# Four engines pinned to the written order instead of five: SyncE's transfers left to the scheduler

## The chip, the cores and the metric

One core of one Trainium2 chip runs the whole program. The metric is device microseconds (us) of that core. A core has four computing engines, called here as the profile calls them: PE (TensorE, matrix multiplication), DVE (VectorE), ACT (ScalarE) and POOL (GpSimd). The fifth, SP (SyncE), computes nothing in this kernel: it issues transfers (DMAs) between the main memory and the on-chip memory. Each engine works through its own list of instructions in a fixed order. An instruction whose inputs are not there yet holds up everything behind it in the same list, on SP as on the others.

## What is computed

Two stages follow each other, all in float32. The first is an attention with a complex decay, for 4 batches and 8 heads, 768 steps, 48 channels:

```python
mag = np.sqrt(a_re * a_re + a_im * a_im)
scale = np.minimum(mag, 0.999) / (mag + 1e-06)
a_re_n, a_im_n = (a_re * scale, a_im * scale)
for t in range(S):
    new_re = ar * S_re - ai * S_im
    new_im = ar * S_im + ai * S_re
    S_re, S_im = (new_re + kv, new_im)          # kv: outer product of k[t] and v[t]
    y[:, :, t] = einsum(q[:, :, t], S_re)
```

The second takes y as x of shape (4, 768, 384) and computes a gated product: a causal convolution over 5 steps and a sigmoid give `gate`, and the output is `(gate * (x @ w_val)) @ w_out`.

## The kernel before, in words

The heads are cut into 10 units, in the order in which they are worked on: units 0, 1, 8 and 9 have 2 heads each, units 2 to 7 have 4. A unit needs five inputs, `ar`, `ai`, `k`, `q` (each loaded by two transfers of line 114) and `v` (three transfers, line 132). The steps of one unit are these:

- `prep_x` (from line 269) turns `ar` and `ai` into logarithms and angles. ACT reads `ar` at line 278 and DVE reads `ai` at line 284; each frees the buffer that it read.
- Sums, angles, sines and exponentials follow (lines 304 to 367).
- `prep_b` (from line 369): DVE multiplies by `k` (line 379) and makes the tile `kx` (line 382); SP writes `kx` to a scratch tensor `kd` in main memory (line 392, two transfers). Then DVE multiplies by `q` (line 379) and makes `qx` in the tile `trig` (line 382).
- `load_kn` (from line 402) reads `kd` back in another layout into a tile `kn`, in two sets for each unit (line 413; two or three transfers each). A set can begin when `kd` has landed and one of three `kn` buffers is free. The transfers of one set write interleaved columns of one tile, and the second waits until the first has landed.
- `transpose` (from line 416): PE transposes `kx` and `qx` (line 430), ACT copies the results into `kq` (line 431). There is one `kx` buffer, so the next unit's `kx` waits until these transposes are done.
- `Attend` works through six chunks of 128 steps: scores on PE (lines 457 and 458), mask on DVE (line 464), output on PE (lines 477 and 480, copied by ACT at 481), and the running state from `kn` and `v` on PE (lines 494 and 495, copied by ACT at 497). `collect` (line 509, issued by POOL) moves the output into the layout of the second stage, whose convolution is on DVE (lines 518 and 521), sigmoid on ACT (529), and products on PE (line 255).

The four inputs `ar`, `ai`, `k`, `q` share six buffers (`LB`, line 80), and `v` has two (`VB`). When the trace of the program is recorded, each step is written in the order of the long string `ORDER` (line 22): one letter is one step of one stream, for instance `L` a load, `N` a `kn` set, `V` a load of `v`. In `move` (line 795) a load is written only after the step that read the buffer six loads earlier. The buffer that it really gets is chosen later, by the scheduler of the framework, among those that are free.

That scheduler goes through the recorded instructions and gives each engine its list. Left alone it puts, on each engine, the instruction first that is ready first by its own estimate of times, and the one written first among those ready. The lines 855 to 866 take this freedom away: they go through all instructions and tie each one to the one before it on the same engine, if the engine is in `IN_ORDER` (lines 35 to 37). Such a tie costs no semaphore on the chip; it fixes the order of the list only.

```python
IN_ORDER = (
    mybir.EngineType.PE, mybir.EngineType.Activation, mybir.EngineType.DVE, mybir.EngineType.SP, mybir.EngineType.Pool
)
```

Of the kernel before, what the change touches and what calls it, by code (L numbers as in the profile page):

```python
# [32 lines left out]
    "MDMOOMMMMMOCCCCCCGMMMMMMMMOOMMO"  # L33
)
IN_ORDER = (
    mybir.EngineType.PE, mybir.EngineType.Activation, mybir.EngineType.DVE, mybir.EngineType.SP, mybir.EngineType.Pool
)
TURN = 2.0 ** 24
RADIAN = 2.0 * PI / 2.0 ** 32 * (1.0 - 2.0 ** -22)
# [962 lines left out]
```

## Time and profile before

| what | value |
|---|---|
| median of 3 runs | 351.83 us (351.12 to 354.74) |
| time of the profiled execution | 351.17 us |
| its span, first to last instruction | 349.4 us |
| PE, DVE, ACT, POOL busy | 269.5, 257.9, 245.7, 60.1 us |
| mean granted clock of PE | 0.924 of full speed |
| moved by DMA | 53.31 MB |

The profile is one execution. "Busy" is the time in which an engine computes; SP has none, so its rows show when it issues transfers. An idle time is shown in brackets with what ended it. "SPq" is SP's list, "L114" is line 114 of the kernel, and `kn<-kd` reads "written: `kn`, read: `kd`". A row with x3 in SP's rows spans three transfers, from the issue of the first to the end of the issue of the third.

### The profile page before, as it was taken

To read this page: it belongs to the slowest core of one execution; us is meant where nothing else is said; L and a number is where in the kernel's file an instruction comes from. 1 tells how busy PE (TensorE), PEld (TensorE's weight loads), DVE (VectorE), ACT (ScalarE), POOL (GpSimd) and SP (SyncE) were. 2 spreads that over 40 slices of the span, in tenths; PEclk is the share of its full clock that TensorE was granted. 3 is DMA by queue.
4 is the path that set the end of the run, shared out by engine and by line. 5 is a ranking of instruction groups with operands and counts; after the bars stand their busy time and mean duration, and the time that the engine had idled before them with its cause. 6 is when DMAs were issued, how large, how long until landed. Compare 5 with 4: busy or idle time off the path is not lost.

```text
span 349.4 us, 8122 instructions
## 1 busy us (share of the span) xinstructions
PE 269.5 (77%) x3234; PEld 210.8 (60%) x3234; DVE 257.9 (74%) x341; ACT 245.7 (70%) x455; POOL 60.1 (17%) x148
## 2 busy tenths in 40 slices
PE   0033757668977999996669999979989999999960
PEld 0023646538866777576458787668779666766530
DVE  4799869995959999929297899577769956476400
ACT  5758789999657899987357989956996457553110
POOL 3000001111023032020212022200342031240210
PEclk9999887956989999999968999996999999999995
DMA  7993576768697851595969403768950441530220
GB/s 203 316 224 112 140 231 182 108 207 221 172 239 200 167 169 48 193 272 170 258 127 208 108 33 102 218 176 259 191 139 26 124 105 46 154 93 2 85 68 7
DMA packets 87804, 53.31 MB, mean 153 GB/s; under 512 B 36432, under 2 KB 84816, under 8 KB 87760
## 3 DMA queue, kind: packets, MB, share of 16 engines
q1 hardware_dynamic: 83664, 43.28, 48.8%
q0 software_dynamic: 4096, 9.44, 9.1%
q8 instruction: 27, 0.44, 0.5%
q14 instruction: 17, 0.14, 0.1%
HBM read 33.83 MB, written 14.16 MB: 137 GB/s over the span
## 4 chain that ended last, share of the span: by engine, by line
DMA 24%; DVE 19%; PE 18%; ACT 16%; issue 9%; SPq 8%; POOL 2%; POOLq 0%; DVEq 0%; ACTq 0%
DMA kn<-kd 14%; SPq L114 4%; ACT L104 4%; PE pt L430 3%; PE pv L255 3%; PE po L255 3%; ACT kq L431 3%; DVE sm L464 3%; DVE z L521 2%; DMA kd<-kx 2%; DVE kx L382 2%; DVE main L379 2%; DMA raw<-in_moe_w_val_dram 2%; SPq L413 2%; PE sc_ps L457 2%
## 5 line engine op out<-in xcount | busy, mean ns | idle before, releaser
L509 POOL DMA_DIRECT2D xT<-y_sb x80 | 40.8, 516 | 156.3 <-ACT y_sb L481 120.8
L431 ACT COPY kq<-pt 96x384 f32<-96x384 f32 x128 | 51.8, 508 | 4.4 <-PE pt L430 4.2
L521 DVE SCALAR_TENSOR_TENSOR z<-xT,cw_sb,z 128x768 f32<-128x768 f32 (+1 forms) x60 | 51.4, 856 | 1.7
L480 PE MATMUL y_ps<-sm,v_in 128*48 128x128 f32 x384 | 44.0, 294 | 10.2 <-DVE sm L464 10.2
L255 PE MATMUL po<-wo_sb,z 128*64 128x384 f32 x288 | 51.2, 488 | 0.0
L255 PE MATMUL pv<-xT,wv_sb 128*64 128x384 f32 x288 | 49.8, 486 | 0.0
L464 DVE TENSOR_TENSOR sm<-sc_ps,mask 128x512 f32<-128x512 f32 (+1 forms) x60 | 34.5, 578 | 15.9 <-PE sc_ps L458 11.8
L430 PE MATMUL pt<-ident,kx 128*96 128x128 f32 x192 | 37.9, 314 | 9.8 <-DVE kx L382 9.5
L457 PE MATMUL sc_ps<-kq 96*64 96x128 f32 x384 | 43.2, 286 | 1.7 <-DVE sm L464 1.7
L477 PE MATMUL y_ps<-kq,S_sb 96*48 96x128 f32 x320 | 38.5, 300 | 7.3 <-ACT y_sb L481 5.1
L458 PE MATMUL sc_ps<-kq 96*64 96x64 f32 x384 | 43.3, 229 | 0.0
L458 PEld LDWEIGHTS sc_ps<-kq 96*64 96x64 f32 x384 | 40.1, 143 | 2.0
L104 ACT ACT_TABLE_LOAD x31 | 39.8, 1283 | 1.3 <-PEq L986 0.8
L430 PE MATMUL pt<-ident,trig 128*96 128x128 f32 x192 | 36.7, 306 | 4.7 <-DVE trig L382 2.8
L457 PEld LDWEIGHTS sc_ps<-kq 96*64 96x64 f32 x384 | 33.6, 145 | 4.6 <-DVE sm L464 2.1
L255 PEld LDWEIGHTS pv<-xT,wv_sb 128*64 128x64 f32 x288 | 25.8, 137 | 16.1
L494 PE MATMUL S_ps<-v_in,kn 128*64 128x48 f32 x320 | 30.0, 233 | 7.2 <-ACT S_sb L497 5.1
L480 PEld LDWEIGHTS y_ps<-sm,v_in 128*48 128x48 f32 x384 | 28.6, 133 | 11.2 <-DVE sm L464 11.2
L481 ACT COPY y_sb<-y_ps 112x256 f32<-112x256 f32 (+1 forms) x60 | 19.5, 324 | 21.9 <-PE y_ps L480 21.6
L255 PEld LDWEIGHTS po<-wo_sb,z 128*64 128x64 f32 x288 | 24.6, 136 | 15.4 <-DVE z L542 1.5
L430 PEld LDWEIGHTS pt<-ident,kx 128*96 128x96 f32 x192 | 24.1, 144 | 14.4 <-issue 11.9
L477 PEld LDWEIGHTS y_ps<-kq,S_sb 96*48 96x48 f32 x320 | 22.6, 132 | 15.6 <-ACT y_sb L481 8.1
(84 smaller groups left out, 487.6 us busy)
## 6 DMA issues: line engine op xcount, KB each, us to landing
kd<-kx SPq DMA_DIRECT2D x12, 576.0 KB, 4.4
out_dram<-ot POOLq DMA_DIRECT2D x24, 192.0 KB, 2.5
ar_in<-in_a_re_dram SPq DMA_DIRECT2D x12, 288.0 KB, 4.5
ai_in<-in_a_im_dram SPq DMA_DIRECT2D x12, 288.0 KB, 5.2
k_in<-in_k_dram SPq DMA_DIRECT2D x12, 288.0 KB, 4.4
q_in<-in_q_dram SPq DMA_DIRECT2D x12, 288.0 KB, 4.4
xT<-y_sb POOLq DMA_DIRECT2D x48, 72.0 KB, 3.2
v_in<-in_v_dram SPq DMA_DIRECT2D x16, 144.0 KB, 5.1
```

The costliest lines, as they stand in the source:

```text
L104: nc.scalar.preload_act_table_set(name)
L255: nc.tensor.matmul(out[c:c + 64], lhsT[:, c:c + 64], rhs, **kw)
L430: nc.tensor.transpose(pt[:C2, j, :], src[:, j, f, h, :], ident)
L431: nc.scalar.copy(tj[:, s, f], pt[:C2].rearrange("c j p -> c p j"))
L457: nc.tensor.matmul(sc[lo:lo + half, h, :], k[:, :half], q, start=True, stop=True)
L458: nc.tensor.matmul(sc[hi:hi + half, h, half:], k[:, half:], q[:, half:], start=True, stop=True)
L464: nc.vector.tensor_tensor(out=two(sm), in0=two(sc[:, :g]), in1=mask[:, :, None, :].to_broadcast([C, 2, g // 2, C]), op=ALU.mult)
L477: nc.tensor.matmul(o, self.S_sb[n - 1][:, h * D:(h + 1) * D], self.part(1, h, n), start=True, stop=False)
L480: nc.tensor.matmul(o, vt[:, h, n], sm[:, h, :], start=(n == 0), stop=True)
L494: nc.tensor.matmul(S_all[:64, cols], kn[:, c0:c0 + 64], vt[:, h, n], **at_h)
L509: XQ.dma_start(out=xTs[b][c0 % P:c0 % P + c2 - c0, c0 // P, EXT + hf * HS:EXT + (hf + 1) * HS], in_=self.y[hf][r0:r0 + c2 - c0, h // 2],)
L521: nc.vector.scalar_tensor_tensor(out=z, in0=xT[:, c, EXT + t0 - t:EXT + t0 - t + n], scalar=cw_sb[:, TAPS - 1 - t, c:c + 1], in1=z, op0=AL ...
```

## The change

SP is taken out of `IN_ORDER`. The loop of lines 855 to 866 then leaves out SP's instructions, and their order is chosen by the scheduler: at each point of its own estimated time, of the transfers that are ready, the one written first. What a transfer waits for (its data, its buffer) stays as it was. PE, ACT, DVE and POOL keep the written order. No instruction is added or removed.

```diff
 IN_ORDER = (
-    mybir.EngineType.PE, mybir.EngineType.Activation, mybir.EngineType.DVE, mybir.EngineType.SP, mybir.EngineType.Pool
+    mybir.EngineType.PE, mybir.EngineType.Activation, mybir.EngineType.DVE, mybir.EngineType.Pool
 )
```

## Rows read from the trace of the kernel before

**Rows 1.** The chain of work that ended last, on the page: its shares of the span by line.

```profile
DMA kn<-kd 14%; SPq L114 4%; ACT L104 4%; PE pt L430 3%; PE pv L255 3%; PE po L255 3%; ACT kq L431 3%; DVE sm L464 3%; DVE z L521 2%; DMA kd<-kx 2%; DVE kx L382 2%; DVE main L379 2%; DMA raw<-in_moe_w_val_dram 2%; SPq L413 2%; PE sc_ps L457 2%
```

**Rows 2.** Waits of SP's own list over the whole span: line, what it waited for, us in total, times, longest.

```profile
SPq L413 <- DMA kn<-kd: 70.3, 20, 6.9
SPq L392 <- DVE kx L382: 44.0, 3, 23.6
...
SPq L392 <- DVE z L542: 18.1, 1, 18.1
...
SPq L114 <- ACT kq L431: 1.8, 2, 1.2
```

**Rows 3.** Waits of all computing engines over the whole span, the two that name a load: us in total, times, longest.

```profile
DVE main L284 <- DMA ai_in<-in_a_im_dram: 21.4, 5, 6.3
...
ACT main L278 <- DMA ar_in<-in_a_re_dram: 13.1, 6, 4.5
```

**Rows 4.** SP's list in order of time: start us, us, line, transfer, count.

```profile
92.48 1.05 SPq L114 DMA_DIRECT2D ar_in<-in_a_re_dram  x2
...
97.34 2.46 SPq L392 DMA_DIRECT2D kd<-kx  x2
...
102.75 8.60 SPq L413 DMA_DIRECT2D kn<-kd  x3
...
122.16 1.00 SPq L114 DMA_DIRECT2D ar_in<-in_a_re_dram  x2
140.85 1.23 SPq L392 DMA_DIRECT2D kd<-kx  x2
144.24 4.33 SPq L413 DMA_DIRECT2D kn<-kd  x3
148.63 1.22 SPq L114 DMA_DIRECT2D ai_in<-in_a_im_dram  x2
...
155.77 8.05 SPq L413 DMA_DIRECT2D kn<-kd  x3
...
165.20 2.72 SPq L114 DMA_DIRECT2D ai_in<-in_a_im_dram  x2
168.03 9.00 SPq L413 DMA_DIRECT2D kn<-kd  x3
177.12 3.68 SPq L132 DMA_DIRECT2D v_in<-in_v_dram  x3
...
219.87 4.25 SPq L413 DMA_DIRECT2D kn<-kd  x3
224.18 1.10 SPq L114 DMA_DIRECT2D ai_in<-in_a_im_dram  x2
```

**Rows 5.** DVE in order of time, the readers of `ai` (L284), `k` and `q` (L379) and the makers of `kx` (L382): start us, us, in brackets the idle time before.

```profile
109.32 1.35 DVE L284 TENSOR_TENSOR main<-tmp,ai_in 128x1152 f32<-128x1152 f32 x1
...
136.88 1.35 DVE L379 TENSOR_TENSOR main<-main,k_in 128x1152 f32<-128x1152 f32 x1
138.26 2.56 DVE L382 TENSOR_TENSOR kx<-trig,main 128x2304 f32<-128x2304 f32 x1
...
141.21 1.35 DVE L379 TENSOR_TENSOR main<-main,q_in 128x1152 f32<-128x1152 f32 x1
...
154.62 1.36 DVE L284 TENSOR_TENSOR main<-tmp,ai_in 128x1152 f32<-128x1152 f32 x1 [6.34 <-DMA ai_in<-in_a_im_dram]
...
157.34 2.56 DVE L382 TENSOR_TENSOR kx<-trig,main 128x2304 f32<-128x2304 f32 x1
...
174.28 1.36 DVE L284 TENSOR_TENSOR main<-tmp,ai_in 128x1152 f32<-128x1152 f32 x1 [6.02 <-DMA ai_in<-in_a_im_dram]
```

**Rows 6.** ACT in order of time, three readers of `ar`.

```profile
49.02 1.16 ACT L278 ACTIVATE main<-ar_in 128x1152 f32<-128x1152 f32 x1 [1.63 <-DMA ar_in<-in_a_re_dram]
...
97.46 1.16 ACT L278 ACTIVATE main<-ar_in 128x1152 f32<-128x1152 f32 x1 [3.42 <-DMA ar_in<-in_a_re_dram]
...
236.59 0.68 ACT L278 ACTIVATE main<-ar_in 128x576 f32<-128x576 f32 x1 [4.53 <-DMA ar_in<-in_a_re_dram]
```

**Rows 7.** Busy time by stretch of 35 us: the stretch, its us, PE, PEld, DVE, ACT and POOL busy with their instructions, granted clock of PE, share of the DMA engines, GB/s.

```profile
105.00:140.00 35.00, 31.99 (x414) 25.12 (x412) 34.10 (x37) 31.30 (x52) 7.16 (x16) 1.00 0.59 145
140.00:175.00 35.00, 27.83 (x363) 20.77 (x358) 22.21 (x21) 24.96 (x45) 6.28 (x14) 0.98 0.79 223
```

**Rows 8.** Waits of PE from 140 to 186 us: us in total, times, longest.

```profile
PE y_ps L480 <- DVE sm L464: 6.5, 2, 4.9
PE S_ps L494 <- DMA v_in<-in_v_dram: 2.0, 2, 1.0
...
PE S_ps L495 <- DMA kn<-kd: 0.5, 1, 0.5
```

**Rows 9.** Waits of PE from 70 to 116 us, the one on `kn`.

```profile
PE S_ps L495 <- DMA kn<-kd: 3.5, 2, 2.7
```

**Rows 10.** PE in order of time: the end of unit 4's transposes, and three instructions with idle time before them.

```profile
98.88 0.34 PE L494 MATMUL S_ps<-v_in,kn 128*64 128x48 f32 x1 [2.57 <-ACT S_sb L497]
...
153.65 0.53 PE L430 MATMUL pt<-ident,trig 128*96 128x128 f32 x3
...
234.75 0.42 PE L480 MATMUL y_ps<-sm,v_in 128*48 128x128 f32 x3 [2.11 <-DVE sm L464]
...
237.53 0.34 PE L494 MATMUL S_ps<-v_in,kn 128*64 128x48 f32 x1 [0.68 <-ACT S_sb L497]
```

## The prediction

> **What bounds the kernel now.** I began with the chain of work that ended last [rows 1]. Its largest single piece is not a computation but the read-back `kn<-kd`, 14% of the span, and SP's list stands in it by name (L114, L413). So I went to the waits of SP's own list [rows 2]. The reader should see two long ones. SP stood 70.3 us at line 413, in 20 waits, until the first transfer of a `kn` set had landed so that the second could follow. And it stood at line 392 until DVE had made a `kx`: 44.0 us and 18.1 us in the two largest entries. While SP stands, nothing behind it goes out, whether it is ready or not. The third view says who pays [rows 3]: DVE waited 21.4 us for `ai`, ACT 13.1 us for `ar`.
>
> Then the stretches. From 105 to 140 us DVE is full (34.10 of 35 us); from 140 to 175 us no engine is: PE 27.83, DVE 22.21, ACT 24.96 [rows 7]. Where all three are idle at once, something outside them sets the pace, and SP's list shows what: after the load of `ar` at 122.16 it stands until the store of `kx` at 140.85, then issues a `kn` set, and only at 148.63 the load of `ai` for which DVE then idles 6.34 us [rows 4, 5].
>
> **Could the load have gone earlier?** It needs a free buffer. The written rule would give it the one of six loads before, which is `q` of unit 4, read at 141.21 [rows 5]. But the rule is not what the chip waits for: the `ar` load at 122.16 went out although the `k` that the rule names was read only at 136.88 [rows 4, 5]. So any free buffer serves, and the last one needed was freed when DVE had read the previous `ai`, at 109.32 + 1.35 = 110.67. The load issued at 148.63 could go right behind the `ar` load, at about 123: 25 us earlier. Likewise the `ai` loads at 165.20 and 224.18 could follow the reads at 154.62 and 174.28 (the first of these itself earlier by then). None of these loads depends on the store or the set that it now stands behind.
>
> **The change part by part.** It removes no transfer and adds none: the issue time on SP stays, about 0.6 us for each transfer (1.22 us for the two at 148.63 [rows 4]), and it is hidden since SP has the waits above to fill. No dependency is changed either. What moves: each load goes out when a buffer is free, past the store of `kx` that waits for DVE and past the second transfer of a `kn` set that waits for the first. I follow four places and take PE's waits as the measure, since PE is the busiest engine and the others feed it.
>
> - From 36 to 70 us, ACT's wait of 1.63 us for `ar` at 49.02 [rows 6].
> - From 70 to 116 us: ACT waits 3.42 us for the `ar` issued at 92.48 behind a `kn` set, and PE waits 2.57 us for ACT [rows 4, 6, 10]; and PE waits 3.5 us for `kn` itself [rows 9], of a set that began at 102.75 because the store before it went out only at 97.34 [rows 4]. Together 6.1 us. Behind this stretch DVE is full [rows 7], so that PE can run ahead of it only in part.
> - From 140 to 186 us: PE waits 6.5 us for DVE's mask, which stands in DVE's list behind the two reads of `ai` that waited 6.34 and 6.02 us [rows 5, 8]; 2.0 us for `v`, issued at 177.12 behind a `kn` set of 9.00 us [rows 4, 8]; and 0.5 us for `kn`. Together 9.0 us. Not all of DVE's 12.4 us comes back: the next `kx`, at 157.34, needs the one `kx` buffer, which PE reads until 153.65 + 0.53 = 154.18 [rows 5, 10]. DVE gains at most 157.34 - 154.18 = 3.2 us there; that is still more than the first of PE's two waits (6.5 - 4.9 = 1.6).
> - From 222 to 245 us: PE waits 2.11 and 0.68 us [rows 10] behind `ai` issued at 224.18 and the `ar` for which ACT waits 4.53 us [rows 4, 6]. Together 2.8 us.
>
> Behind 245 us I credit nothing: the loads end, and the last of ACT's waits for `ar` is that at 236.59.
>
> **What it costs.** A load that goes earlier is earlier in the DMA queue too, ahead of the transfers that matter most. DVE frees `k` before it makes `kx` and `q` a little after it, at 141.21 + 1.35 for a store at 140.85 [rows 4, 5]. So the next loads of `k` and `q` now tend to enter just before the store and just before the `kn` set. Sets with other transfers issued directly ahead took 8.60, 8.05 and 9.00 us; those issued into a quiet queue 4.33 and 4.25 [rows 4]. The price is 8.60 - 4.33 = 4.3 us for a set. The bounds for one set are 0 (it is loaded already, as three of the five shown are) and 4.3. The two quiet ones, at 144.24 and 219.87, can lose it. At the first PE has transposes until 154.18, and the set was issued by 148.57; most of the 4.3 is hidden there. At the second I found no cover. I take 4.0 for both together.
>
> The Trainium skill (DMA: Bandwidth & Descriptors, section "Queues, rings and completion order") says that each DMA engine consumes the descriptors of a queue in ring order, so that a load entered first passes first; by that rule this price is systematic, and the sum would be that of the slower rival below. The trace agrees with it as far as 8.05 to 9.00 against 4.3 us goes.
>
> The scheduler's order rests on its own estimate. If a buffer comes free on the chip later than estimated, SP now stands at a load with a `kn` set behind it. No such order is in this trace. The nearest rows are waits of line 114 for a reader's end: 1.8 us in two [rows 2]. Bounds 0 and, where whole units drift apart, the 18.1 us of the longest wait but one of a store; I take 1.8, as the readers are tied to the same four orders as before.
>
> **The sum.** Half of the first two places, because of the full DVE behind them: (1.63 + 6.1)/2 = 3.9. The third and fourth in full: 9.0 + 2.8 = 11.8. Less 4.0 and 1.8: a gain of 9.9 us. The profiled execution took 351.17 us (span 349.4, and 1.8 around it), so 341.3; the median of the runs lies 0.7 above that execution, so 342.0. The upper bound of the gain is all four places without a price, 1.6 + 6.1 + 9.0 + 2.8 = 19.5: 332.
>
> **The rivals.**
> - *New waits take the place of the old.* PE then gains only where it waits on a transfer by name in the third place, 2.0 + 0.5 us, and the rest turns into waits on the `kx` buffer, ACT's copies or the full DVE. For it: PE has idle times behind ACT and DVE, and the two feed each other in a fixed order. Against it: in 140 to 175 us all three are idle together [rows 7]. Time: 351.8 - 2.5 = 349.3.
> - *Slower: the loads get ahead of the `kn` sets.* Place: the first set of units 2 to 7. Price: 4.3 us each if none is covered, 6 x 4.3 = 25.8 against a gain before prices of 3.9 + 11.8 = 15.7, so 351.8 + 10.1 = 362. It decides from 15.7/6 = 2.6 us for each unit on, and it is over 1% slower from (15.7 + 3.5)/6 = 3.2: 355 to 362. For it: `kn<-kd` is the largest piece of the chain [rows 1]. Against it: three of the five sets shown pay this price now.
> - *The order hardly changes*, if the scheduler's estimate makes each transfer ready in the written order. Against it: `ai` could go 25 us earlier than it does, more than any estimate should miss. Time: 351.8.
>
> **How the numbers follow.** Forecast, 335 to 348: 0.55. Most of the upper bound, 331 to 335: 0.11. New waits 0.13 and unchanged order 0.04, both within 1%. Slower, 355 to 362: 0.17. About 1% (3.5 us) is what a measurement of this kernel can tell from no change. So faster by over 1%: 0.66; within 1%: 0.17; slower: 0.17. The range must reach past the cases around no change and the edge of the slower one: 331 to 356. The likeliest case alone has 335 to 348.
>
> **What would show it.** Right: DVE's waits for `ai` fall from 21.4 to under 6 us and ACT's for `ar` from 13.1 to under 6; the load of `ai` of unit 6 goes out before the store of unit 4's `kx`; SP's 70.3 us at line 413 shrink to under half, with other transfers issued between those of one set; PE's 9.0 us between 140 and 186 us fall to about 3. Wrong: `kn` sets that all take 8 us and more with longer waits of PE at line 494 or 495 (slower rival); DVE's waits gone but as long ones at line 382 for PE, or of PE for ACT (new waits); SP standing at line 114 or 132 for a buffer while a `kx` is ready (the estimate is off). What would make the prediction wrong above all is the price for the sets, which only two quiet ones bound.

## The result, and the profile after

| what | before | after |
|---|---|---|
| median of the runs, same chip | 351.48 us (350.68 to 354.74, 4 runs) | 333.12 us (331.88 to 334.39, 4 runs) |
| span of the profiled execution | 349.4 us | 331.2 us |
| PE, DVE, ACT busy | 269.5, 257.9, 245.7 us | 264.8, 257.4, 246.3 us |

The ratio is 0.9462, 95% interval 0.9391 to 0.9532: faster by 18.4 us. The forecast was 342.0 with a range of 331 to 356, so the sign is right and the time lies in the range, but the gain is nearly twice the 9.9 us of the sum and close to its upper bound of 19.5. The likeliest case, 335 to 348, was missed: 333.12 lies in the case from 331 to 335, which had a chance of 0.11. DVE and ACT compute as long as before, and on them the 18 us are idle time that went away; PE computes 4.7 us less, at a mean granted clock of 0.940 for 0.924. The lists of PE, DVE, ACT and POOL have the same instructions in the same order in both programs. Only SP's list differs.

The chain that ended last: by engine before, by engine after, and by line after, which answers to [rows 1]:

```profile
DMA 24%; DVE 19%; PE 18%; ACT 16%; issue 9%; SPq 8%; POOL 2%; POOLq 0%; DVEq 0%; ACTq 0%
PE 33%; DVE 23%; ACT 16%; DMA 12%; issue 9%; POOL 2%; SPq 2%; POOLq 0%; ACTq 0%; DVEq 0%
PE pt L430 9%; PE pv L255 6%; PE po L255 4%; DMA kn<-kd 4%; ACT L104 3%; PE sc_ps L457 3%; PE y_ps L480 3%; DMA xT<-y_sb 3%; DVE sm L464 3%; DVE main L249 3%; DMA kd<-kx 3%; DVE main L379 3%; DMA raw<-in_moe_w_val_dram 3%; PE y_ps L477 2%; DVE main L318 2%
```

The read-back `kn<-kd` falls from 14% to 4%, and SP's own pieces from 8% to 2%; PE's own work now leads. SP's waits after, in us, times, longest, beside [rows 2]:

```profile
SPq L114 <- DVE main L379: 53.5, 4, 21.7
...
SPq L413 <- DMA kn<-kd: 31.7, 17, 3.6
...
```

SP still stands a lot, but at other things: the long waits are now at a load (line 114) whose buffer DVE has not read yet. Behind the longest of them stands a store that is not ready either: it ends at 200.41, and the `kx` for the store is made at 200.42 + 2.56 (rows below). The waits inside the sets are under half (31.7 for 70.3). The waits of the computing engines after, answering to [rows 3], and one that was 3.1 us before:

```profile
DVE kx L382 <- PE pt L430: 9.1, 3, 3.3
...
ACT main L278 <- DMA ar_in<-in_a_re_dram: 2.9, 2, 1.6
...
DVE main L284 <- DMA ai_in<-in_a_im_dram: 0.3, 1, 0.3
```

The waits for loads are gone (21.4 to 0.3, 13.1 to 2.9). In place of part of them DVE waits for the one `kx` buffer. SP's list after, in time order (start, us, line, transfer, count), beside [rows 4]:

```profile
111.87 1.64 SPq L114 DMA_DIRECT2D ai_in<-in_a_im_dram  x2
133.35 0.92 SPq L114 DMA_DIRECT2D k_in<-in_k_dram  x2
135.94 2.28 SPq L392 DMA_DIRECT2D kd<-kx  x2
141.07 0.37 SPq L413 DMA_DIRECT2D kn<-kd  x1
141.54 0.98 SPq L114 DMA_DIRECT2D q_in<-in_q_dram  x2
144.20 1.29 SPq L413 DMA_DIRECT2D kn<-kd  x2
...
146.78 0.59 SPq L413 DMA_DIRECT2D kn<-kd  x1
...
152.00 1.24 SPq L413 DMA_DIRECT2D kn<-kd  x2
153.34 2.08 SPq L132 DMA_DIRECT2D v_in<-in_v_dram  x2
155.51 1.39 SPq L392 DMA_DIRECT2D kd<-kx  x2
...
200.41 0.97 SPq L114 DMA_DIRECT2D k_in<-in_k_dram  x2
203.00 1.24 SPq L392 DMA_DIRECT2D kd<-kx  x2
206.44 0.37 SPq L413 DMA_DIRECT2D kn<-kd  x1
```

The `ai` load that stood behind the store and the set until 148.63 goes out at 111.87, and in the gap between the first and the second transfer of a set a load now goes out. The price is seen too: unit 5's store waits until 155.51 although its `kx` was made by 151.39 (148.83 + 2.56, in the next rows), behind the second set of unit 4 and two transfers of `v`. The same instructions of DVE as in [rows 5], and those of the later places, after:

```profile
133.36 2.56 DVE L382 TENSOR_TENSOR kx<-trig,main 128x2304 f32<-128x2304 f32 x1
...
143.29 1.35 DVE L284 TENSOR_TENSOR main<-tmp,ai_in 128x1152 f32<-128x1152 f32 x1
...
148.83 2.56 DVE L382 TENSOR_TENSOR kx<-trig,main 128x2304 f32<-128x2304 f32 x1 [2.92 <-PE pt L430]
...
200.42 2.56 DVE L382 TENSOR_TENSOR kx<-trig,main 128x2304 f32<-128x2304 f32 x1
...
210.01 0.75 DVE L284 TENSOR_TENSOR main<-tmp,ai_in 128x576 f32<-128x576 f32 x1
214.89 2.56 DVE L382 TENSOR_TENSOR kx<-trig,main 128x2304 f32<-128x2304 f32 x1 [2.85 <-PE pt L430]
...
241.56 0.62 DVE L518 TENSOR_SCALAR z<-xT,cw_sb 128x768 f32<-128x768 f32 x1 [2.88 <-DMA xT<-y_sb]
```

And their like in the kernel before, as far as [rows 5] does not have them:

```profile
213.87 2.56 DVE L382 TENSOR_TENSOR kx<-trig,main 128x2304 f32<-128x2304 f32 x1
...
229.42 0.76 DVE L284 TENSOR_TENSOR main<-tmp,ai_in 128x576 f32<-128x576 f32 x1 [5.87 <-DMA ai_in<-in_a_im_dram]
...
244.65 0.56 DVE L249 TENSOR_TENSOR main<-main 128x384 f32<-128x384 f32 x1 [2.23 <-ACT main L312]
...
260.42 0.62 DVE L518 TENSOR_SCALAR z<-xT,cw_sb 128x768 f32<-128x768 f32 x1 [3.21 <-DMA xT<-y_sb]
```

Since DVE's list is the same in both, the distance between the starts of one instruction is the lead at that point. It is 138.26 - 133.36 = 4.9 us at unit 4's `kx`, 213.87 - 200.42 = 13.45 at unit 6's, and 260.42 - 241.56 = 18.86 after the last load; from there to DVE's last instruction it stays at 18.86. So the whole difference arises before 262 us, in the places that the prediction followed: it began 1.3 us late in this execution (the load of the second stage's weights landed later, in a part of SP's list that is the same in both), gained 6.2 in the first two places (-1.3 to 4.9), 8.5 in the third, 5.4 in the fourth.

Stretches after, as in [rows 7], and PE's waits from 140 to 186 us, as in [rows 8]:

```profile
105.00:140.00 35.00, 32.94 (x402) 23.52 (x400) 33.48 (x38) 31.04 (x42) 4.44 (x9) 0.95 0.51 140
140.00:175.00 35.00, 31.11 (x401) 25.62 (x398) 28.60 (x27) 27.73 (x57) 9.64 (x21) 0.91 0.86 238
```

```profile
PE S_ps L495 <- DMA kn<-kd: 3.0, 1, 3.0
...
```

In the stretch in which all engines were idle together, PE, DVE and ACT now work 3.3, 6.4 and 2.8 us longer. PE's waits for the mask and for `v` are gone; a wait of 3.0 us for unit 5's `kn` is new.

### The profile page after: what moved, and what is told of

Its sections match the earlier page's. It is cut to its first block, busy times and chain, and to the rows that moved or that the text cites. A ratio compares the mean times of both kernels' runs of the same rounds, so it can differ in the third digit from the quotient of the medians.

```text
span 331.2 us, 8130 instructions
## 1 busy us (share of the span) xinstructions
PE 264.8 (80%) x3234; PEld 205.4 (62%) x3234; DVE 257.4 (78%) x341; ACT 246.3 (74%) x455; POOL 59.8 (18%) x148
## 4 chain that ended last, share of the span: by engine, by line
PE 33%; DVE 23%; ACT 16%; DMA 12%; issue 9%; POOL 2%; SPq 2%; POOLq 0%; ACTq 0%; DVEq 0%
PE pt L430 9%; PE pv L255 6%; PE po L255 4%; DMA kn<-kd 4%; ACT L104 3%; PE sc_ps L457 3%; PE y_ps L480 3%; DMA xT<-y_sb 3%; DVE sm L464 3%; DVE main L249 3%; DMA kd<-kx 3%; DVE main L379 3%; DMA raw<-in_moe_w_val_dram 3%; PE y_ps L477 2%; DVE main L318 2%
## 5 line engine op out<-in xcount | busy, mean ns | idle before, releaser
L255 PE MATMUL pv<-xT,wv_sb 128*64 128x384 f32 x288 | 51.4, 500 | 0.0
L430 PE MATMUL pt<-ident,kx 128*96 128x128 f32 x192 | 37.2, 309 | 9.9 <-DVE kx L382 9.5
L480 PE MATMUL y_ps<-sm,v_in 128*48 128x128 f32 x384 | 42.0, 281 | 3.2 <-DVE sm L464 3.2
L458 PE MATMUL sc_ps<-kq 96*64 96x64 f32 x384 | 42.6, 227 | 0.0
L477 PE MATMUL y_ps<-kq,S_sb 96*48 96x128 f32 x320 | 36.6, 286 | 6.5 <-ACT y_sb L481 3.6
L458 PEld LDWEIGHTS sc_ps<-kq 96*64 96x64 f32 x384 | 38.6, 141 | 1.7
L457 PEld LDWEIGHTS sc_ps<-kq 96*64 96x64 f32 x384 | 32.3, 142 | 5.5 <-DVE sm L464 2.9
L481 ACT COPY y_sb<-y_ps 112x256 f32<-112x256 f32 (+1 forms) x60 | 19.5, 326 | 19.7 <-PE y_ps L480 19.3
L477 PEld LDWEIGHTS y_ps<-kq,S_sb 96*48 96x48 f32 x320 | 21.6, 125 | 14.5 <-ACT y_sb L481 5.9
L480 PEld LDWEIGHTS y_ps<-sm,v_in 128*48 128x48 f32 x384 | 27.5, 127 | 4.2 <-DVE sm L464 4.0
L813 POOL DMA_DIRECT2D out_dram<-ot x24 | 13.5, 561 | 92.3 <-ACT ot L576 67.2
```

The source lines that it names most:

```text
L255: nc.tensor.matmul(out[c:c + 64], lhsT[:, c:c + 64], rhs, **kw)
L430: nc.tensor.transpose(pt[:C2, j, :], src[:, j, f, h, :], ident)
L457: nc.tensor.matmul(sc[lo:lo + half, h, :], k[:, :half], q, start=True, stop=True)
L458: nc.tensor.matmul(sc[hi:hi + half, h, half:], k[:, half:], q[:, half:], start=True, stop=True)
L477: nc.tensor.matmul(o, self.S_sb[n - 1][:, h * D:(h + 1) * D], self.part(1, h, n), start=True, stop=False)
L480: nc.tensor.matmul(o, vt[:, h, n], sm[:, h, :], start=(n == 0), stop=True)
```

## The experiments

Two theories went into the first runs. **A**: the gain is that of the loads, which no longer stand behind a blocked transfer. **B**: it is that of the `kn` sets, stores and `v`, which go out earlier and are read by PE directly. All ratios are to the kernel before, run on the same chip, with the 95% interval.

**Only the loads freed.** On the kernel before; all else on SP stays tied.

```diff
...
-            nc.sync.dma_start(
+            free.append(nc.sync.dma_start(
...
-            )
+            ).ins.name)
...
-        if ins.engine not in IN_ORDER:
+        if ins.engine not in IN_ORDER or ins.name in free:
```

> Kernel before, but only the loads of ar, ai, k and q (line 114) are left to the scheduler; the stores of kx, the kn sets and v keep their written order among themselves on SP. Theory A: the gain comes from those loads no longer standing behind a blocked store or set. Then nearly all of it is here: 333 to 339 us, DVE's waits for ai under 4 us in all, PE's 2 us for v left over. Theory B: the gain comes from the kn sets, which are issued closer together. Then little of it is here: 346 to 350 us.

Measured 335.82 us, ratio 0.9537 (0.9473 to 0.9601). A's range holds, B's does not. The profiled execution is the longest of the four (339.27 us) and so is no measure of the median, but it shows what the loads alone leave: PE waits 8.8 us for `v`, which is still tied behind a set, and not the 2 us expected.

**Only the `kn` sets freed.** The same edit around the transfer of line 413 in place of that of line 114.

> Kernel before, but only the transfers of the kn sets (line 413) are left to the scheduler; loads, stores of kx and v keep their written order among themselves. A load still stands behind a store of kx, but no longer behind the wait inside a set. Theory A: part of the gain, as the loads of ai go out some 4 us earlier where DVE lost 6 us: 336 to 343 us, DVE's waits for ai some 1 to 2 us at each of three places. Theory B: all of it, 331 to 336 us.

Measured 335.84 us, 0.9538 (0.9477 to 0.9599): the same as with the loads freed. It lies just under A's range and just inside B's, so by its number this run decides for B as much as for A. DVE's waits for `ai` fell to 4.7 us though no load was freed. A load comes earlier either way: it may pass the set, or the rest of the set may fall behind it; here only the store still holds it.

**No wait inside a set, order kept.** On the kernel before, with all five engines tied: the two halves of a set get separate columns of the `kn` tile, so that no transfer of a set waits for another.

```diff
-        kn = flat[:, :N * g * C2].rearrange("i (n x) -> i n x", n=N)
+        kn = flat[:, :N * g * C2].rearrange("i (k n x) -> i k n x", k=2, n=N)
...
-                nc.sync.dma_start(out=kn[i0:i0 + n, :, cols], in_=src[i1:i1 + n, :, cols])
+                nc.sync.dma_start(out=kn[i0:i0 + n, 2 * h // g], in_=src[i1:i1 + n, :, cols])
...
-                c0 = (n % HN * self.g + h) * C2
+                c0 = ((2 * h // self.g * min(HN, NCH - 1 - n // HN * HN) + n % HN) * (self.g // 2) + h % (self.g // 2)) * C2
```

> Kernel before with all five engines in the written order, but a kn tile keeps the two halves of the heads in separate columns, so that the transfers of one set no longer overlap and none waits for another of its set. SP's list is the same but for one transfer at its end. It takes away the 70.3 us of line 413 and leaves the waits for kx. Theory A: the load of ai for which DVE lost 6.34 us goes out about 3 us earlier, and so at the other places: 339 to 345 us. Theory B (the sets as such): 333 to 338 us. If SP's waits at the sets had no part in it: 350 to 353 us.

Measured 333.51 us, 0.9479 (0.9413 to 0.9544). A's number missed; B's holds. The written order, with its 70.3 us of waits at line 413 gone, is as fast as the free order. A wait of SP and its list in this run:

```profile
SPq L392 <- DVE kx L382: 53.1, 5, 26.1
```

```profile
137.38 1.23 SPq L392 DMA_DIRECT2D kd<-kx  x2
140.77 1.69 SPq L413 DMA_DIRECT2D kn<-kd  x3
142.50 1.15 SPq L114 DMA_DIRECT2D ai_in<-in_a_im_dram  x2
```

The `ai` load still stands behind the store and the set, until 142.50, and yet DVE no longer waits for it there: its read, at 148.19, waits 3.38 us for ACT's copies instead. The load needed to go some 6 us earlier than its 148.63 of before, not the 25 that were open to it. So A and B are not two causes but two links of one chain: DVE waits for `ai`, `ai` stands behind the set, the set stands in itself. Cutting any link frees most of the time. SP's long waits for a `kx` are not such a link: they are still there (53.1 us for 44.0 before), with the same loads behind them.

**The change and the layout together.**

> Changed kernel (SP left to the scheduler) with the separate columns of the third kernel. Theory A: the loads are early already; what is left to gain are PE's waits for kn, 4.5 us in the changed kernel's profile, and a little behind them: 328 to 332 us. Theory B: the sets still set the pace: 318 to 327 us. If loads and sets now compete for the DMA engines: 333 us or more.

Measured 331.43 us, 0.9418 (0.9347 to 0.9489). A's number holds, B's misses. It lies 1.7 us under the change and 2.1 under the layout alone, with intervals that overlap: with one link cut, a further gain from the other is not clear of the spread.

**Everything freed but the loads.** The names of the loads in `free`, and a tie only for them.

```diff
-        if ins.engine in before:
+        if ins.engine in before and (ins.engine != mybir.EngineType.SP or ins.name in free):
```

> The counterpart of the first experiment: only the loads of ar, ai, k and q stay behind what is written before them on SP; stores of kx, kn sets and v are left to the scheduler. Theory A (the gain is that of the loads alone): the loads of ai are as late as before, DVE waits 15 us or more for them, 344 to 350 us, with at most the 2 to 5 us of v and kn gained. Theory B (stores, sets and v bring it): 333 to 338 us.

Measured 343.54 us, 0.9797 (0.9723 to 0.987), just under A's range and far from B's. DVE's waits for `ai` stay at 17.9 us (5 times, longest 6.7), among them one of 5.49 at 220.23, the like of the 5.87 at 229.42 before.

**PE's waits, or its clock?** In the fourth place PE's granted clock fell in the kernel before: its windows (stretch, us, busy of PE, PEld, DVE, ACT, POOL, granted clock, DMA share, GB/s):

```profile
234.00:240.00 6.00, 4.57 (x56) 4.36 (x58) 6.00 (x8) 2.04 (x5) 0.00 (x0) 0.59 1.01 306
240.00:246.00 6.00, 6.00 (x100) 5.79 (x97) 3.77 (x6) 5.08 (x11) 1.40 (x3) 0.84 0.65 181
```

PE had waited 2.11 us just ahead [rows 10], and a score matmul of 96x128 just behind the wait takes 0.42 us, against 0.27 where the full 2.4 GHz are granted. Was the clock what made the fourth place worth 5.4 us instead of the 2.8 of the sum? The first try put 18 matmuls that add zeros (two instructions each in the trace) ahead of the first output of unit 6, in the bank of the running state.

```diff
-            att[u].output(n)
+            steps(iter([keep_busy() for i in range(18 * ((u, n) == (6, 0)))])); att[u].output(n)
```

> Kernel before in the written order, plus 18 matmuls that add zero (line 238), issued by PE right before the output of unit 6's first chunk, that is in the idle time of 2.11 us that stands at 234.75. If the granted clock of PE falls there because PE was idle, then the stretch from 234 to 246 us is granted 0.9 or more in place of 0.59 and 0.84, PE's next 160 instructions take some 3 us less, and the time is 348 to 350 us. If the low clock there has another cause (load on the DMA engines, the transposes before), the granted clock stays and the time is 351 to 353 us.

Measured 357.03 us, 1.0183 (1.0106 to 1.0259): both numbers missed.

```profile
235.59 6.16 PE L238 MATMUL S_ps<-dmat,zero 128*64 128x128 f32 x35 [4.80 <-ACT S_sb L497]
```

The added matmuls themselves waited 4.80 us for ACT's copy out of that bank and then ran at a granted clock of 0.50 (234 to 240 us), the 1.2 GHz level. The run made a new wait and tests nothing of the clock. The second try puts twelve of them into the bank of the output, which is free there:

```diff
-            S_all[:64, 512 - KEEP:], zero,
+            y_ps[0][:64, 512 - KEEP:], zero,
```

> The kernel before, with twelve matmuls that add zeros put into PE's list ahead of the first output of unit 6, in the output's own bank, so that they can run in the 2.11 us in which PE stands there for sm; they add zeros, so nothing computed changes. If the low granted clock of the following stretch (0.59 and 0.84 in the kernel before) cost the time of the fourth place, the eighty matmuls from instruction 2080 on need about 4 us in place of 6.5 and the kernel takes 348.5 to 349.5. If that stretch is long for another reason, the time stays at 351 to 352 or rises by what the added matmuls need, up to 354.

Measured 351.82 us, 0.9981 (0.9943 to 1.0019): no change, and the interval leaves room for a gain of 2.0 us at most, of the 5.4 - 2.8 = 2.6 in question. The windows of this run:

```profile
234.00:240.00 6.00, 4.56 (x97) 4.30 (x97) 6.00 (x7) 2.94 (x7) 0.00 (x0) 1.00 0.97 305
240.00:246.00 6.00, 5.96 (x95) 5.19 (x93) 5.05 (x9) 5.97 (x15) 3.21 (x8) 1.00 0.69 191
```

The clock stays at 1.00, PE's standing of 2.11 us is filled, and the kernel takes as long as before: DVE is busy for 6.00 of 6.00 us from 234 to 240 in both, behind its wait for `ai` (5.81 us in this run). PE's slow clock ran in the shadow of DVE. It is not the cause.

**Is a load ahead of a set dear?** On the changed kernel, the `q` load of unit u+2 tied behind the first set of unit u.

```diff
+            ); tied.extend([(u - 2, ins.ins)] * (nm == "q" and u >= 2))
...
+                last[u, hn] = nc.sync.dma_start(out=kn[i0:i0 + n, :, cols], in_=src[i1:i1 + n, :, cols]).ins
...
+    steps(iter([tc.add_manual_dep(ins, last[u, 0].name, nosync, reason="behind the set") for u, ins in tied]))
```

> Changed kernel, but the load of q of the unit after next is held until the first kn set has been issued whole (an order on SP's list, no semaphore). It tests the price of 4.0 us that the prediction took off for loads that enter the DMA queue ahead of the sets. If the price is real: the sets are shorter, PE's waits for kn (4.5 us in the changed kernel) shrink by 2 us or more, 328 to 331 us. If it is hidden: within 1 us of the changed kernel in the same job, 332 to 334 us. If q becomes late: 335 us or more.

Measured 330.04 us, 0.9392 (0.9306 to 0.9479); the unedited change beside it, as a control:

> The changed kernel itself in the same job, as the measure for the one before: 331 to 335 us.

333.0 us, 0.9486 (0.9417 to 0.9555). The number of a real price hit, the reason not: PE's waits for `kn` were to shrink by 2 us and are 4.5 us, against 4.4 in the control. Unit 4's first set with the load held, where a transfer of `v` took the gap, then in the control with the load in between:

```profile
139.91 0.37 SPq L413 DMA_DIRECT2D kn<-kd  x1
140.38 0.43 SPq L132 DMA_DIRECT2D v_in<-in_v_dram  x1
143.06 1.29 SPq L413 DMA_DIRECT2D kn<-kd  x2
144.44 1.10 SPq L114 DMA_DIRECT2D q_in<-in_q_dram  x2
```

```profile
140.14 0.37 SPq L413 DMA_DIRECT2D kn<-kd  x1
140.61 0.98 SPq L114 DMA_DIRECT2D q_in<-in_q_dram  x2
143.19 1.29 SPq L413 DMA_DIRECT2D kn<-kd  x2
```

The set takes 143.06 + 1.29 - 139.91 = 4.44 us on SP with the transfer of `v` and 143.19 + 1.29 - 140.14 = 4.34 with the load. The empty gap is seen in the kernel before, where the same set took 4.33 [rows 4]. So what goes out in the gap uses time in which SP stands anyway; the last transfer of the set landed 8.2 us after the issue of the first in the control, against 7.4 in the kernel before. The intervals of the two runs overlap; whether the 3 us are real stays open.

**Unit 5's store ahead of unit 4's second set.** On the changed kernel, against the late store at 155.51.

```diff
+            last[u] = nc.sync.dma_start(
...
+    steps(iter([tc.add_manual_dep(ins, last[u + 1].name, nosync, reason="behind the store") for u, hn, ins in tied if (u, hn) == (4, 1)]))
```

> The changed kernel, with the second set of unit 4 held behind the store of unit 5's kx in SyncE's list. In the changed kernel that store is issued 4.1 us after its kx is ready, since SyncE stands in the waits of unit 4's second set, and PE then waits 2.98 us for unit 5's first kn. If the wait is owed to the order on SyncE, unit 5's set lands about 4 us earlier, the 2.98 us goes and the time falls to 329 to 331. If the set is late for the traffic of that stretch, or if unit 4's second set is now late in its turn, the time stays at 332 to 335.

Measured 340.27 us, 0.9657 (0.96 to 0.9713): slower than the change by about 6 us, worse than either expectation.

```profile
148.01 5.16 SPq L132 DMA_DIRECT2D v_in<-in_v_dram  x3
153.27 2.25 SPq L392 DMA_DIRECT2D kd<-kx  x2
155.62 2.90 SPq L413 DMA_DIRECT2D kn<-kd  x2
...
160.28 3.26 SPq L413 DMA_DIRECT2D kn<-kd  x5
```

```profile
160.40 0.23 PE L494 MATMUL S_ps<-v_in,kn 128*64 128x48 f32 x1 [3.06 <-DMA kn<-kd]
164.07 0.29 PE L495 MATMUL S_ps<-v_in,kn 128*33 128x48 f32 x1 [3.28 <-DMA kn<-kd]
```

With the set held back, the three transfers of a `v` moved ahead of the store and took 5.16 us of SP; the store came at 153.27, only 2 us sooner, and unit 4's second set began at 155.62 in place of 146.78. PE now waits for both. One wait was exchanged for two. The same edit with the layout that has no waits in a set:

> The edit of the run before together with the kn layout in which no transfer of a set waits for another. If both losses are real and stand apart, 327 to 330. If one covers the other, as in the runs that freed one half of the list, 330 to 333.

337.05 us, 0.9559 (0.9503 to 0.9615): both expectations missed; the layout wins back some 3 us of the loss, with intervals that overlap. And the held `q` load with that layout:

> The changed kernel with the q load held behind the first set and with the kn layout in which no transfer of a set waits for another. If the 3 us that the held load gave were owed to shorter sets, they come again on top of the layout: 327 to 329. If they were only the spread of the runs, 330 to 333, what the layout gives alone.

330.91 us, 0.9403 (0.9358 to 0.9447): what the layout gives alone, so the held load adds nothing that can be told. It and the two runs at 330.04 and 331.43 lie 2 to 3 us under the change, but no interval parts from the change's own.

**By place.** The gain over the kernel before in us, in the profiled executions, read as the lead of the same DVE instruction at 28, 142, 206 and 262 us of the kernel before:

```text
run                          first two   third   fourth
the change                      6.2       8.5      5.4
the change again                6.7       9.6      5.5
only kn sets freed              5.0       4.9      4.5
no wait in a set, order kept    4.3       8.5      5.5
all freed but the loads         6.9       2.8      0.6
store of unit 5 first           6.5       2.8      5.5
fill at the output             -0.5       2.5      0.8
```

The last row has the list of the kernel before up to the fourth place, so its 2.5 in the third is what two executions differ by. It lies in one wait of DVE, here in the kernel before:

```profile
193.71 0.96 DVE L249 TENSOR_TENSOR main<-main 128x768 f32<-128x768 f32 x1 [2.47 <-ACT main L312]
```

The wait is 2.08 us in the change, 1.15 in the change again and 0.00 in the other five rows. As it is gone in the fill run with an unchanged list, it is not counted as a gain: next to nothing is left of the 2.8 of two rows, 2.5 of the 4.9, 6.0 of the 8.5 of the run without waits, and some 8 of the change's 8.5. The run with only the loads freed is left out for its long execution; its waits of PE for `v` fall into the third place (6.54 us at 173.22, 2.26 at 176.14).

Read this way, the first two places do not need the loads freed (with the loads late, too, DVE's 2.28 us for `ai` at 52.41 are gone), the fourth needs them to come earlier (0.6 where they do not), and the third needs both the loads and the sets in time.

## Why the prediction was right, and where its sizes were not

**The mechanism** was right: loads that stand on SP behind transfers they do not depend on. All signs named for it came: `ai` waits 0.3 us and `ar` waits 2.9 (under 6 each), `ai` at 111.87, ahead of the store, 70.3 us at line 413 to 31.7 with other transfers between, PE's 9.0 us gone with a new wait of 3.0 in their place. That everything but the loads gives only 343.54 shows that the loads have to come earlier for the larger part of the gain; that they need not be freed themselves is shown by the 335.84 of the `kn` sets. What the prediction did not see is which of the two blocks that it named counts. Taking away only the waits inside the sets, in the written order, gives 333.51; the stores that wait for `kx` may stay where they are.

**First two places: 3.9 predicted, 6.2 measured.** The step that failed is the halving "because of the full DVE behind them". DVE was full only after it had itself waited for PE, at 102.62 in the kernel before:

```profile
52.41 1.36 DVE L284 TENSOR_TENSOR main<-tmp,ai_in 128x1152 f32<-128x1152 f32 x1 [2.28 <-DMA ai_in<-in_a_im_dram]
...
102.62 0.69 DVE L464 TENSOR_TENSOR sm<-sc_ps,mask 128x512 f32<-128x512 f32 x1 [4.01 <-PE sc_ps L458]
```

So PE's waits there reached DVE, and what PE won, DVE won too. Unhalved, the term was 7.7. DVE's own two long waits, the 4.01 and the 2.28 for `ai`, which the prediction did not list, make 6.3, and both are gone in the change.

**Third place: 9.0 predicted, 8.5 measured**, with the price in it. That the two agree is in part luck. PE's 6.5, 2.0 and 0.5 us went and 3.0 us for `kn` came, so by PE's waits, the prediction's own measure, the place is worth 6.0. The 8.5 is DVE's: of its 6.34 + 6.02 us for `ai`, 2.92 came back as the wait for the `kx` buffer at 148.83 and 1.10 as a wait for scores at 153.09, which leaves 8.3. The bound by that buffer, at most 3.2 us for DVE at that point, nearly held: the lead there is 157.34 - 148.83 = 8.5, which is 3.6 above that at unit 4's `kx`. That is the rival of the new waits in small.

**Fourth place: 2.8 predicted, 5.4 measured.** The step that failed is the measure, "PE's waits". DVE had lost 5.87 us for `ai` there, and behind it 2.23 and 1.76 for ACT; DVE set the pace, and PE's idle time was short because its clock had fallen and it worked longer on the same rows. By DVE: 5.87 + 2.23 less the new `kx` wait of 2.85 is 5.25, near the 5.4; all its idle time in the place fell from 13.4 to 8.0. The fill run shows that speeding PE there gives nothing, and the run with late loads that the place is lost with the `ai` load.

**The prices: 4.0 + 1.8 predicted.** The first had a right mechanism and a wrong size. Its 4.3 us for a set came from the three longest sets; five others of the same list, also directly behind loads (from 115.01, 180.91, 226.49, 239.46 and 248.90), took 5.86, 4.63, 5.47, 5.32 and 6.93 us, which is 0.3 to 2.6 above the quiet 4.33. A load directly ahead of the store does delay the set: unit 4's first `kn` goes out 141.07 - 135.94 = 5.1 us after its store began, against 144.24 - 140.85 = 3.4 before [rows 4] and 206.44 - 203.00 = 3.4 at unit 6: 1.7 us, at one unit of the two, and there PE's transposes hid it. In the control it is 140.14 - 135.37 = 4.8. Both stores had a `k` load ahead of them; that of unit 4 moves 288 KB a transfer and landed at 139.09, in the middle of the store, that of unit 6 half as much, landed at 203.60. Unit 4's set itself takes no longer on SP with a load inside it (4.34 against 4.33 before). With 3.2 us for each of six units needed, the slower rival is far off. The Trainium skill (DMA: Bandwidth & Descriptors, section "Queues, rings and completion order") says that each DMA engine consumes descriptors in ring order; the 1.7 us agree with it. The prediction's reading of it, that the price is then systematic, is not what the runs show: at unit 6 nothing was lost. The second price, the scheduler's estimate, is seen as the store of unit 5, 155.51 - 151.39 = 4.1 us late, with PE's wait of 3.0 us for its `kn` behind it. It came in another way than told: SP stood not for a buffer but inside unit 4's second set until 152.00, and then issued the rest of that set and `v` first. That the one causes the other was only argued: the run that moved the store made it 2 us earlier and the waits longer.

The sum with what was measured: 6.2 + 8.5 + 5.4 - 1.3 (the late start) = 18.8, against a difference of the two spans of 349.4 - 331.2 = 18.2. The four are leads of one list, so that they add up is bookkeeping and no test of the causes.

## What to carry to other kernels

An issuing engine's list is a queue like any other: a transfer that waits there delays all that stand behind it, so the time of a late load is to be looked for in the wait of the instruction in front of it. Before freeing an order, look for the wait that blocks the list and ask whether it is needed; here separate columns in a tile did as much as a free order. Where several engines feed each other, measure a place by the engine whose lead reaches the end (the same instruction in both traces), not by the waits of the busiest one.

## What the runs showed of the hardware

PE's granted clock fell to 0.59 behind 2.11 us of standing in the kernel before, and stayed at 1.00 when those 2.11 us were filled with matmuls, without any gain for the kernel; matmuls that followed a wait of 4.80 us ran at 0.50. And two executions of the same lists differ by some 2.5 us over one place of 64 us (the fill run up to its third place, in one wait of DVE for ACT), although the medians of a kernel in different jobs agree within 0.9 us (351.18 to 352.05).
